# One core: x and u are split into two fp16 parts and transposed by DMA, where TensorE transposed them in f32

## The chip, the core and the metric

The kernel runs on one core of a Trainium2 chip. That core has a matrix engine (TensorE, PE in the profile; PEld is its weight load), a vector engine (VectorE, DVE), an activation engine (ScalarE, ACT), a general engine (GpSimd, POOL) and an engine that here only issues DMA transfers (SyncE, SP). Each executes its own list of instructions in order, and semaphores tie the lists together. The metric is the time of one execution on the device in microseconds (us); less is better.

## The reference

Two stages for 4 batches of 768 tokens. The first is attention in 8 heads of 64, in which a query sees only the keys of its own bucket; the second mixes channels and tokens of the result `x` (768 x 512 for each batch):

```python
    mask = q_bucket[:, :, :, None] == k_bucket[:, :, None, :]
    scores = scale * np.matmul(q, k.transpose(0, 1, 3, 2))
    scores = np.where(mask, scores, -1000000000.0)
    ...
    x = np.ascontiguousarray(attn_out.transpose(0, 2, 1, 3)).reshape(B, S, H * D)
    ...
    theta = x @ w_theta
    cos_t, sin_t = (np.cos(theta), np.sin(theta))
    zr = x * cos_t
    zi = x * sin_t
    yr = np.einsum('ts,bsd->btd', w_tok_r, zr)
    yi = np.einsum('ts,bsd->btd', w_tok_i, zi)
    u = x + (yr + yi)
    return (u + np.maximum(u @ w_ch, 0.0)).astype(np.float32)
```

All inputs are float64 or float32 arrays of random numbers; the output is float32.

## The kernel before

**Tiling.** The 768 tokens of a batch are 6 tiles of 128 partitions, the 512 channels 4 chunks of 128. Products are made nearly exact by splitting each operand into a high and a low part and summing three products (high x high, high x low, low x high). A "tile" of a product is thus 4 chunks x 3 terms = 12 matmuls of 128x128 by 512 columns for theta (`ps_th`) and for the channel product (`ps_r`), and 6 token tiles x 2 (real, imaginary) x 3 = 36 for the token product (`py`).

**Attention** (`prep_qk`, `prep_v`, `maxima`, `step`): for each head `sq` are scores whose row maxima DVE takes (`mc`, L721), `st` the scores once more in transposed form, `pf` the exponential on ACT (L799), two parts `p` of it on ACT (L805) and POOL (L811), and `po` the product with the values. DVE divides and writes the result into `x` (`rc` L849, `x` L855).

**The second stage** (`moe`), for each batch: `transposed` has PE transpose a 128x512 tile of x into PSUM (`pt_x`, L900, 4 instructions), ACT copies it as the high part (`h_x`, L905, format fp32r), DVE subtracts for the low part (`l_x`, L909); `project` multiplies by the theta weights (`ps_th`); ACT rounds to whole turns (`n`, L941), DVE takes the rest (L944), ACT and DVE the magnitude; `trig` takes cosine and sine for 3 tiles at once (L966, L967), DVE multiplies by x (`f`, L978), and `z` is split in two fp16 parts (L983, L985, L989). `token` sums `py`, DVE adds it to x (L1017, this is u), u is transposed and split as x was (`pt_u`, `h_u`, `l_u`), multiplied by the channel weights (`ps_r`), DVE takes the ReLU and adds (L1024), and SP stores (L1027).

**Weights** arrive as 64-bit floats and are rebuilt as f32 on DVE and ACT (`widened`, L381, L385, L390, L391). The two token weights come in 6 row tiles `t0` to `t5` (`prep_wtok`), get a power-of-two scale for each row (L354 to L356, L394), are transposed on PE (`pwt`, L439) and split into fp16 (`wtk`). The theta and channel weights (`wth`, `wch`) are held in fp32r, split chunk by chunk (`split_weight`).

**What sets the order.** `issue_all` builds each engine's list before the program is made: a list scheduler with its own durations takes, on each engine that it holds to be free, the ready operation of least priority number. The priority numbers are the constants at the end of the file (`TH0` for theta, `Y0` for py, `W0` for token weights, and so on), in units of one attention step. `Slot` objects are buffers: `xt` (2) holds a transposed and split tile, `m` (4 banks of PSUM) the accumulators of the attention and of `moe`, `tmp` (3) f32 tiles. Theta and py of a batch are put among the attention of the next; those of batch 3 stand alone at the end.

Of the kernel before, what the change touches and what calls it, by code (L numbers as in the profile page):

```python
# [34 lines left out]
def lsh_attention_moe_kernel(ctx: ExitStack, tc: tile.TileContext, q, k, v, proj, w_theta, w_tok_r, w_tok_i, w_ch, aff, out):  # L35
    nc = tc.nc
# [312 lines left out]
    sinv = const.tile([P, T], F32, name="sinv")  # L349
# [14 lines left out]
    def widened(srcs, n, nm, tag, prio, am=None, stage="x", by=1.0, scaled=None):  # L364
# [5 lines left out]
        def load():  # L370
# [31 lines left out]
    wready = {"th": [], "ch": [], "tk": []}

    def split_weight(src, dst, c, cols, nm, tag, stage, prio, by=1.0):
        lo, n = cols
        k_ = n / DM
        t, g, sz = widened([src[c * P : (c + 1) * P, lo : lo + n].bitcast(U32)], n, f"{nm}{c}_{lo}", tag, prio, stage=stage, by=by)
        dh, dl = (d[:, c, lo : lo + n] for d in dst)
        h_ = op("wh", prio, on("ACT", 100 + 420 * k_, lambda: ACT.activation(dh, t["w"][:, 0], AF.Copy)), [g], [sz])

        def low(eng):
            return lambda: eng.tensor_tensor(dl, t["w"][:, 0], dh.bitcast(F32), ALU.subtract)

        wready[nm].append(h_)
        wready[nm].append(op("wl", prio, {"POOL": (130 + 1100 * k_, low(POOL)), "DVE": (65 + 535 * k_, low(DVE))}, [h_], [sz]))

    def prep_wtok(tau, prio):
        am = const.tile([P, 1], F32, name=f"wam_{tau}")
        def scale(t):
# [5 lines left out]
            S, f"t{tau}", "z0" if tau >= LATE else f"z{tau % 2}", prio, am, "z1" if tau >= LATE else "x", scaled=scale,  # L425
# [3 lines left out]
        for c0 in range(0, 2 * T, TC):  # L429
            def chunk(c0=c0):  # L430
# [12 lines left out]
                wready["tk"].append(op("wtl", prio, on("DVE", 66 + 133.5 * TC, lambda: DVE.tensor_tensor(lo, u["pt"], hi, ALU.subtract)), [e], [sm_]))  # L443
# [419 lines left out]
    def moe(b, G):  # L863
# [28 lines left out]
        def transposed(src, nm, prio, deps, kind):  # L892
            u = {}
            sm_, make = acc(f"pt_{nm}", kind)
            sxt = Slot("xt")

            def tr():
                u["pt"] = make().rearrange("p (c n) -> p c n", c=NC)
                for c in range(NC):
                    PE.transpose(u["pt"][:, c], src()[:, c * P : (c + 1) * P], ident)  # L900

            def high():
                u["hi"] = mp.tile([P, NC, P], F32R, tag="h" + sxt.tag, name=f"h_{nm}")
                u["lo"] = mp.tile([P, NC, P], F32R, tag="l" + sxt.tag, name=f"l_{nm}")
                ACT.activation(u["hi"], u["pt"], AF.Copy)  # L905
# [3 lines left out]
            c = op("xl", prio, on("DVE", 600, lambda: DVE.tensor_tensor(u["lo"], u["pt"], u["hi"].bitcast(F32), ALU.subtract)), [b_], [sm_, sxt])  # L909
# [22 lines left out]
        for tt in range(T):  # L932
            def theta(tt=tt):
                prio = G + at("TH0", b) + at("TH1", b) * tt
                u, deps, sxt = transposed(lambda: tl[b][:, tt], f"x{b}_{tt}", prio, xready[b][tt // 2], "x")
                res, pe, sm_ = project(u, deps, sxt, wth, f"th{b}_{tt}", prio, wready["th"], "p")
                s1 = Slot("tmp")

                def turns():
                    u["n"] = tmp(f"n_{b}_{tt}", s1)  # L940
                    ACT.activation(u["n"], res["ps"], AF.Identity, bias=magic)  # L941
# [16 lines left out]
        for t0, t1 in GROUPS[GR1 if b == B - 1 else GR]:  # L958
            def trig(t0=t0, t1=t1):
# [4 lines left out]
                def go():  # L964
                    c_, s_ = (t["zw"][r][:, sl].rearrange("p t d -> p (t d)") for r in range(2))
                    ACT.activation(c_, c_, AF.Sin, bias=hpi, scale=-TURN)  # L966
                    ACT.activation(s_, s_, AF.Sin, scale=-TURN)  # L967
# [210 lines left out]
```

## Time and profile before

| what | us |
|---|---|
| time, median of 3 runs | 806.96 |
| the 3 runs | 805.57, 808.13, 806.96 |
| the profiled execution, its own time | 808.25 |
| its span, first to last instruction | 806.1 |
| PE, busy in the span | 732.8 |
| ACT, busy | 552.1 |
| DVE, busy | 547.6 |
| POOL, busy | 473.9 |

The span is 2.15 us shorter than the execution's own time. A busy PE is not one at its peak: consecutive matmuls overlap, so the mean duration of one is longer than the distance from one to the next. That distance is read from the chain of waits, which counts each stretch once. The granted PE clock was 0.972 of full speed in the mean.

### The profile page before, as it was taken

The page shows a single profiled execution, that of the slowest core. Times are in us where ns is not written, and L with a number is a line of the kernel's source. Part 1 is how long each engine was busy: PE and PEld are TensorE (multiplying, and loading weights), DVE is VectorE, ACT ScalarE, POOL GpSimd, SP SyncE. Part 2 cuts the span into 40 slices and gives each one's busy share as a digit, 9 for nine tenths or more (in the row PEclk, how much of TensorE's full clock was granted, in tenths as well). Part 3 has the DMA queues.
Part 4 walks back from the last instruction along what each step waited for, and adds up shares of the span by engine and source line. Part 5 has one row for each costly group of instructions (what it writes and reads, how often), then busy time and mean ns, then how long its engine had stood idle before and what let it go on. Part 6 is the DMA issues. An engine that isn't in the chain of part 4 may idle for free.

```text
span 806.1 us, 17749 instructions
## 1 busy us (share of the span) xinstructions
PE 732.8 (91%) x6760; PEld 472.2 (59%) x6760; DVE 547.6 (68%) x1027; ACT 552.1 (68%) x983; POOL 473.9 (59%) x496
## 2 busy tenths in 40 slices
PE   2578697779899999999899999999899999999998
PEld 1246465447555656767556666668556666675456
DVE  7989999895688746685786655684696755236413
ACT  5488899888787754898887564778796654657101
POOL 4168889687659724695569653765667564631200
PEclk9988999999899999999899999999899999999999
DMA  7354454433103232323003220332004110000002
GB/s 219 87 152 145 135 160 143 130 88 84 38 15 109 66 98 66 98 74 88 27 21 103 80 70 29 101 84 69 21 21 115 46 47 14 15 14 1 1 1 78
DMA packets 35268, 59.52 MB, mean 74 GB/s; under 512 B 7456, under 2 KB 24944, under 8 KB 35184
## 3 DMA queue, kind: packets, MB, share of 16 engines
q1 hardware_dynamic: 35184, 58.40, 25.3%
q8 instruction: 53, 0.87, 0.5%
q14 instruction: 31, 0.25, 0.1%
HBM read 32.51 MB, written 6.29 MB: 48 GB/s over the span
## 4 chain that ended last, share of the span: by engine, by line
PE 69%; DVE 13%; ACT 7%; issue 3%; POOL 3%; DMA 3%; SPq 1%; ACTq 0%; DVEq 0%; POOLq 0%
PE py L78 21%; PE st L78 12%; PE po L78 11%; PE ps_r L78 8%; PE ps_th L78 8%; PE sq L78 5%; DVE mc L721 4%; ACT pf L799 3%; DVE hl L577 1%; POOL p L811 1%; ACT p L805 1%; PE pt_u L900 1%; DVE f L978 1%; PE pt_x L900 1%; PE pb L78 1%
## 5 line engine op out<-in xcount | busy, mean ns | idle before, releaser
L811 POOL TENSOR_TENSOR p<-pf,p 128x512 f16<-128x512 f32 x288 | 365.0, 1290 | 143.3 <-ACT p L805 80.0
L78 PE MATMUL py<-z,wtk 128*128 128x512 f16 x864 | 218.2, 385 | 0.5 <-DVE z L989 0.3
L721 DVE TENSOR_REDUCE mc<-sq 128x1 f32<-128x512 f32 (+1 forms) x288 | 188.8, 681 | 40.8 <-PE sq L78 40.0
L799 ACT ACTIVATE pf<-st 128x512 f32<-128x512 f32 x288 | 163.1, 592 | 75.7 <-PE st L78 66.2
L78 PE MATMUL st<-qt,kt 108*128 108x512 f16 (+3 forms) x768 | 169.9, 338 | 24.7 <-ACT pf L799 23.2
L805 ACT ACTIVATE p<-pf 128x512 f16<-128x512 f32 x288 | 170.8, 628 | 18.2 <-PE po L78 16.8
L78 PEld LDWEIGHTS <-p 128*128 128x128 f16 x3456 | 141.6, 99 | 44.1 <-issue 11.0
L78 PE MATMUL po<-vv,p 128*128 128x65 f16 (+1 forms) x3456 | 154.7, 195 | 3.0 <-POOL p L811 2.4
L78 PEld LDWEIGHTS <-wtk 128*128 128x128 f16 x864 | 82.5, 99 | 85.5 <-issue 9.7
L78 PE MATMUL sq<-kt,qt 108*128 108x256 f16 (+1 forms) x384 | 105.7, 337 | 27.1 <-DVE mc L721 18.2
L78 PEld LDWEIGHTS <-kt 108*128 108x128 f16 (+1 forms) x768 | 72.2, 101 | 74.9 <-issue 42.1
L989 POOL TENSOR_TENSOR z<-f,z 128x512 f16<-128x512 f32 x38 | 50.9, 1348 | 71.2 <-ACT z L983 54.2
L78 PEld LDWEIGHTS <-qt 108*128 108x128 f16 x384 | 35.5, 101 | 51.0 <-issue 30.0
L78 PE MATMUL ps_th<-wth,h_x 128*128 128x512 f32 x192 | 64.2, 416 | 1.2 <-DVE z L944 0.8
L78 PE MATMUL ps_r<-wch,h_u 128*128 128x512 f32 x192 | 63.0, 409 | 0.8 <-DVE l_u L909 0.8
L978 DVE SCALAR_TENSOR_TENSOR f<-x,zsc,z 128x512 f32<-128x512 f32 x48 | 56.2, 1208 | 8.8 <-ACT z L966 4.8
L1017 DVE SCALAR_TENSOR_TENSOR x<-py,sw,x 128x512 f32<-128x512 f32 x24 | 17.9, 746 | 48.7 <-PE py L78 48.7
L1024 DVE SCALAR_TENSOR_TENSOR x<-ps_r,x 128x512 f32<-128x512 f32 x24 | 16.6, 691 | 47.3 <-PE ps_r L78 47.3
L905 ACT ACTIVATE h_u<-pt_u 128x512 fp32r<-128x512 f32 x24 | 14.1, 592 | 50.4 <-PE pt_u L900 33.8
L78 PEld LDWEIGHTS ps_th<-wth,h_x 128*128 128x128 f32 x192 | 36.3, 194 | 10.6 <-DVE z L944 1.3
L78 PEld LDWEIGHTS ps_r<-wch,h_u 128*128 128x128 f32 x192 | 35.0, 188 | 10.5 <-DVE l_u L909 2.4
L577 DVE SCALAR_TENSOR_TENSOR hl<-raw,sc,hl 128x768 f16<-128x768 f32 x32 | 40.2, 1266 | 0.0
(128 smaller groups left out, 904.3 us busy)
## 6 DMA issues: line engine op xcount, KB each, us to landing
raw<-in_q_dram SPq DMA_DIRECT2D x16, 384.0 KB
raw<-in_k_dram SPq DMA_DIRECT2D x16, 384.0 KB
vb<-in_v_dram SPq DMA_DIRECT2D x16, 384.0 KB
out_dram<-x SPq DMA_DIRECT2D x24, 256.0 KB
qt<-hl SPq DMA_DIRECT2D x31, 192.0 KB
kt<-hl SPq DMA_DIRECT2D x31, 192.0 KB
w_t<-in_moe_w_tok_r_dram SPq DMA_DIRECT2D x6, 768.0 KB
w_t<-in_moe_w_tok_i_dram SPq DMA_DIRECT2D x6, 768.0 KB
```

What stands on the lines that cost most here:

```text
L78: PE.matmul(out_, l, r, start=start, stop=stop, skip_group_check=True)
L577: DVE.scalar_tensor_tensor(t["hl"][:, 1, i], t["raw", i], t["sc"][:, 2 + i : 3 + i], t["hl"][:, 0, i], ALU.mult, ALU.subtract)
L721: DVE.tensor_reduce(col()[:, cs], u["sq"], AX.X, ALU.max)
L799: ACT.activation(wide("pf", spf, F32), u["st"], AF.Exp, scale=1.0 / (UNIT * math.sqrt(D)))
L805: ACT.activation(o_, u["pf"], AF.Copy)
L811: return lambda: eng.tensor_tensor(wide("p2", sp2, F16), u["pf"], u["p1"], ALU.subtract)
L900: PE.transpose(u["pt"][:, c], src()[:, c * P : (c + 1) * P], ident)
L905: ACT.activation(u["hi"], u["pt"], AF.Copy)
L978: DVE.scalar_tensor_tensor(u["f"], tl[b][:, tt], zsc[:, b : b + 1], t["zw"][r][:, tt], ALU.mult, ALU.mult)
L989: return lambda: eng.tensor_tensor(t["z"][r, 1][:, tt], u["f"], t["z"][r, 0][:, tt], ALU.subtract)
L1017: DVE.scalar_tensor_tensor(tl[b][:, to], res["py"], t["sw"][:, to : to + 1], tl[b][:, to], ALU.mult, ALU.add)
L1024: DVE.scalar_tensor_tensor(tl[b][:, to], r_["ps"], 0.0, tl[b][:, to], ALU.max, ALU.add)
```

## The change

1. **x and u are split before they are transposed.** `transposed` writes into a tile `s` two fp16 parts of the scaled 128x512 tile: the high part on ACT or DVE, the low part (scaled x minus high part) on DVE. Both read x in SBUF. One DMA transpose on SP's queue then turns `s` (128 rows of 8 blocks of 128) into `t`. PE's transposes, their PSUM banks and their copies are gone. `s` has 2 buffers (`xt`), `t` 2 more (`xd`).
2. **Theta and channel weights become scaled fp16.** `prep_weight` gathers all of a weight in f32, takes its sum of magnitudes, a power-of-two scale from one small matmul (`pw`), and then splits into fp16 on ACT and DVE. The scales go into `mg`, `ns`, `su` and `qu`, small DVE operations once for each batch.
3. **ReLU on ACT.** `relu` (ACT, from PSUM, scaled) writes an f32 tile, `fin` (DVE or POOL) adds it to u.
4. **Late token weights.** Tiles `t4` and `t5` have buffers of their own (`wx`, `wz`), and py of batch 0 waits, for each output tile, only for the weights of that tile.
5. **The order is made anew**: other constants, and an offset for each kind of operation and batch (`OFF`).

```diff
-    wth = [wp.tile([P, NC, DM], F32R, name=f"wth{i}") for i in range(2)]
-    wch = [wp.tile([P, NC, DM], F32R, name=f"wch{i}") for i in range(2)]
+    wth = [wp.tile([P, NC, DM], F16, name=f"wth{i}") for i in range(2)]
+    wch = [wp.tile([P, NC, DM], F16, name=f"wch{i}") for i in range(2)]
...
-            S, f"t{tau}", "z0" if tau >= LATE else f"z{tau % 2}", prio, am, "z1" if tau >= LATE else "x", scaled=scale,
+            S, f"t{tau}", "wz" if tau >= LATE else f"z{tau % 2}", prio, am, "wx" if tau >= LATE else "x", scaled=scale,
...
-            def tr():
-                u["pt"] = make().rearrange("p (c n) -> p c n", c=NC)
-                for c in range(NC):
-                    PE.transpose(u["pt"][:, c], src()[:, c * P : (c + 1) * P], ident)
...
-            a = op("xtr", prio, on("PE", 440, tr), deps, [sm_, sx])
-            b_ = op("xh", prio, on("ACT", 480, high), [a], [sm_, sxt])
-            c = op("xl", prio, on("DVE", 600, lambda: DVE.tensor_tensor(u["lo"], u["pt"], u["hi"].bitcast(F32), ALU.subtract)), [b_], [sm_, sxt])
+                    if e == "ACT":
+                        ACT.activation(u["s"][:, 0], src(), AF.Copy, scale=sc())
+                    else:
+                        DVE.tensor_scalar(u["s"][:, 0], src(), sc(), None, ALU.mult)
...
+                DVE.scalar_tensor_tensor(u["s"][:, 1], src(), sc(), u["s"][:, 0], ALU.mult, ALU.subtract)
...
+                nc.sync.dma_start_transpose(u["t"].rearrange("p i c n -> p (i c) n"), u["s"].rearrange("p i d -> p (i d)"))
+
+            a = op("xh", prio, {"ACT": (580, high("ACT")), "DVE": (340, high("DVE"))}, deps, [sx, sxs])
+            c = op("xl", prio, on("DVE", 610, low), [a], [sx, sxs])
+            d = op("xturn", prio, on("SP", [(600, 500000)], turn), [c], [sxs, sxt])
...
-                        mm(res["ps"], u[a][:, c], w[bb][:, c], n == 0, n == len(terms) - 1)
+                        mm(res["ps"], u["t"][:, a, c], w[bb][:, c], n == 0, n == len(terms) - 1)
...
-                    DVE.scalar_tensor_tensor(tl[b][:, to], r_["ps"], 0.0, tl[b][:, to], ALU.max, ALU.add)
+                    ACT.activation(v_["r"], r_["ps"], AF.Relu, scale=t["qu"][:, to : to + 1])
...
+                    return lambda: eng.tensor_tensor(tl[b][:, to], v_["r"], tl[b][:, to], ALU.add)
...
-LATE = 6
+LATE = 4
```

**The order, place 1: the last token weight on DVE.** In the names the first number is the batch: `mc_0_6` is head 6 of batch 0, `wf_t5` token weight tile 5. Before, its rebuilding stands among the maxima of batch 0:

```order
L721 TENSOR_REDUCE mc_0_6_1818<-sq_0_6_6_1862 128x1
L381 TENSOR_SCALAR wf_t5_1755<-w64_t5_1752 128x1536
L516 SCALAR_TENSOR_TENSOR mt_0_3_1790<-pm_0_3_1871,vsc_105,mh_0_3_1879 1x2x64
L385 SCALAR_TENSOR_TENSOR wf_t5_1755<-w64_t5_1752,wf_t5_1755 128x1536
L721 TENSOR_REDUCE mc_0_6_1818<-sq_0_6_7_1869 128x1
```

In the changed kernel it stands about 80 rows later, with the maxima of batch 1 and the first tile of x:

```order
L608 SCALAR_TENSOR_TENSOR hl_1_1_2160<-raw1_1_1_2080,sc_1_1_2161,hl_1_1_2160 128x768
L386 TENSOR_SCALAR wf_t5_2633<-w64_t5_2630 128x1536
L880 RECIPROCAL rc_0_7_1_2838<-po_0_7_0_2587 128x6
L752 TENSOR_REDUCE mc_1_1_2713<-sq_1_1_3_2828 128x1
L886 SCALAR_TENSOR_TENSOR x_0_828<-po_0_7_0_2587,vinv_109,rc_0_7_1_2838 128x6x64
L917 TENSOR_SCALAR sw_0_2727<-sinv_101,zinv_111 128x1
L965 SCALAR_TENSOR_TENSOR s_x0_0_2852<-x_0_828,zsc_112,s_x0_0_2852 128x512
```

Tile 5 (and the two channel chunks that stood ahead of theta) has moved behind the end of batch 0's attention.

**Place 2: SP's list at the end.** `t_x3_0` is the transposed tile 0 of x of batch 3, `t_u3_0` that of u, `out_0_dram` the output. Of the changed kernel:

```order
L969 DMA_TRANSPOSE t_x3_0_11280<-s_x3_0_11270 128x8x128
L969 DMA_TRANSPOSE t_x3_1_11305<-s_x3_1_11272 128x8x128
L1098 DMA out_0_dram<-x_2_6168 128x512
L969 DMA_TRANSPOSE t_x3_2_11332<-s_x3_2_11312 128x8x128
L969 DMA_TRANSPOSE t_x3_3_11360<-s_x3_3_11325 128x8x128
L969 DMA_TRANSPOSE t_x3_4_11396<-s_x3_4_11385 128x8x128
L969 DMA_TRANSPOSE t_x3_5_11418<-s_x3_5_11402 128x8x128
L969 DMA_TRANSPOSE t_u3_0_11591<-s_u3_0_11580 128x8x128
L969 DMA_TRANSPOSE t_u3_1_11605<-s_u3_1_11596 128x8x128
L969 DMA_TRANSPOSE t_u3_2_11654<-s_u3_2_11639 128x8x128
```

Before, SP's list held only stores there. With two buffers for `t`, `t_x3_2` waits until PE has done the 12 matmuls of `ps_th3_0`, and so on by twos.

**Place 3: DVE's last rows.** Before, the last u tiles are split long after their `py` is done:

```order
L1024 SCALAR_TENSOR_TENSOR x_3_9078<-ps_r3_3_11879,x_3_9078 128x512
L909 TENSOR_TENSOR l_u3_1_11903<-pt_u3_1_11871,h_u3_1_11902 128x512
L1024 SCALAR_TENSOR_TENSOR x_3_9078<-ps_r3_2_11898,x_3_9078 128x512
L909 TENSOR_TENSOR l_u3_0_11922<-pt_u3_0_11844,h_u3_0_11921 128x512
L1024 SCALAR_TENSOR_TENSOR x_3_9078<-ps_r3_1_11917,x_3_9078 128x512
L1024 SCALAR_TENSOR_TENSOR x_3_9078<-ps_r3_0_11936,x_3_9078 128x512
```

In the changed kernel each `py` is followed by its split, and three additions stand at the end:

```order
L1081 SCALAR_TENSOR_TENSOR x_3_9044<-py_3_5_11768,sw_3_11153,x_3_9044 128x512
L965 SCALAR_TENSOR_TENSOR s_u3_5_11819<-x_3_9044,su_3_11154,s_u3_5_11819 128x512
L1094 TENSOR_TENSOR x_3_9044<-rl_3_3_11832,x_3_9044 128x512
L1094 TENSOR_TENSOR x_3_9044<-rl_3_4_11847,x_3_9044 128x512
L1094 TENSOR_TENSOR x_3_9044<-rl_3_5_11864,x_3_9044 128x512
```

Between the end of `py_3_5` and the first matmul of `ps_r3_5` PE's list now holds `ps_r3_3` and `ps_r3_4`, 24 matmuls; before, `ps_r` of all six tiles stood behind the last `py`.

More of the change, by code (lines that the diff above doesn't have):

```diff
@@ L362, in root_scale, with widened @@
         DVE.tensor_scalar(r.bitcast(U32), inv.bitcast(U32), MASK, None, ALU.bitwise_xor)
-    def widened(srcs, n, nm, tag, prio, am=None, stage="x", by=1.0, scaled=None):
+    def widened(srcs, n, nm, tag, prio, am=None, stage="x", by=1.0, scaled=None, into=None, hold=()):
         m = len(srcs)
@@ L398, in widened @@
             "DVE": (60 + 535 * k_, lambda: DVE.tensor_tensor(t["f"], t["f"], t["sg"], ALU.mult)),
-        }, [d, t["abs"]], [sz])
+        }, [d, t["abs"]], [sz] + hold)
         return t, g, sz
[L402 to L415, printed above, removed]
+    wready = {"th": [], "ch": [], "tk": [[] for _ in range(T)]}
@@ new lines, in prep_weight, with into, joined, total @@
+    def prep_weight(src, dst, nm, n, tag, stage, prio, step, by=1.0):
+        u = {}
+        sf, sa = Slot("wf"), Slot("m")
+        sums = const.tile([P, NC * DM // n], F32, name=f"wsum_{nm}")
+        col = const.tile([P, 1], F32, name=f"wcol_{nm}")
+        done = []
+        for c in range(NC):
+            for lo in range(0, DM, n):
+                def into(c=c, lo=lo):
+                    if "f" not in u:
+                        u["f"] = mp.tile([P, NC, DM], F32, tag=sf.tag, name=f"wf_{nm}")
+                    return u["f"][:, c, lo : lo + n]
+                i = (c * DM + lo) // n
+                t, g, sz = widened(
+                    [src[c * P : (c + 1) * P, lo : lo + n].bitcast(U32)], n, f"{nm}{c}_{lo}", tag, prio + step * i, sums[:, i : i + 1], stage=stage, by=by, into=into, hold=[sf]
+                )
+                done.append(g)
+        def joined():
+            DVE.tensor_reduce(col, sums, AX.X, ALU.add)
+            DVE.tensor_scalar(col, col, 2.0**-14, col, ALU.mult, ALU.mult)
+            DVE.tensor_scalar(col, col, 2.0**-14, None, ALU.mult)
+        def total():
+            u["pa"] = bank(sa, [P, 1], f"pw_{nm}")
+            mm(u["pa"], ones, col, True, True)
+        last_ = prio + step * (NC * DM // n - 1)
+        a = op("wcol", last_, on("DVE", 450, joined), done)
+        a = op("wall", last_, on("PE", 60, total), [a], [sa])
+        r = op("wcsc", last_, on("DVE", 520, lambda: root_scale(u["pa"], csc[nm], cinv[nm])), [a], [sa])
+        for c in range(NC):
+            dh, dl = (d[:, c] for d in dst)
+            h_ = op("wh", last_ + 0.01 * c, on("ACT", 600, lambda c=c, dh=dh: ACT.activation(dh, u["f"][:, c], AF.Copy, scale=csc[nm])), [r], [sf])
+            wready[nm].append(h_)
+            wready[nm].append(op("wl", last_ + 0.01 * c, on("DVE", 600, lambda c=c, dh=dh, dl=dl: DVE.scalar_tensor_tensor(dl, u["f"][:, c], csc[nm], dh, ALU.mult, ALU.subtract)), [h_], [sf]))
@@ L1036, in lsh_attention_moe_kernel @@
         prep_wtok(tau, W0 + WS * tau if tau < LATE else WL0 + WLS * (tau - LATE))
-    for c in range(NC):
-        split_weight(w_theta, wth, c, (0, DM), "th", "z0", "x", WTH + WTS * c, 1.0 / TWO_PI)
-        for half in range(2):
-            split_weight(w_ch, wch, c, (half * DM // 2, DM // 2), "ch", "tmp", "tmp", WC + WCS * (c + 0.5 * half))
+    prep_weight(w_theta, wth, "th", DM, "z0", "x", WTH, WTS, 1.0 / TWO_PI)
+    prep_weight(w_ch, wch, "ch", DM // 2, "tmp", "tmp", WC, WCS * 0.5)
     g = 0
@@ L1089 @@
 GR = 0
-PEN = 0.031
+PEN = 0.904
 GR1 = 0
```

224 lines of the change are left out of this document (132 added, 92 removed), and 38 rows, old and new, of the table OFF.

## The prediction

> **What bounds the kernel now.** I read the busy times first, then the chain of waits by engine, then the busy times stage by stage.
>
> ```profile
> PE 732.8 (91%) x6760; PEld 472.2 (59%) x6760; DVE 547.6 (68%) x1027; ACT 552.1 (68%) x983; POOL 473.9 (59%) x496
> ```
> ```profile
> PE 69%; DVE 13%; ACT 7%; issue 3%; POOL 3%; DMA 3%; SPq 1%; ACTq 0%; DVEq 0%; POOLq 0%
> ```
> ```profile
> core 0: us, PE busy (x) PEld busy (x) DVE busy (x) ACT busy (x) POOL busy (x), PEclk, DMA share, GB/s
> 0.00:189.00 189.00, 134.70 (x1452) 86.22 (x1453) 168.81 (x325) 151.51 (x273) 134.27 (x142) 0.94 0.47 140
> 189.00:371.00 182.00, 175.32 (x1675) 114.00 (x1675) 128.47 (x247) 134.63 (x249) 116.72 (x125) 0.98 0.26 73
> 371.00:548.00 177.00, 173.92 (x1673) 113.05 (x1672) 118.60 (x230) 126.32 (x227) 112.16 (x120) 0.98 0.24 66
> 548.00:713.00 165.00, 161.27 (x1538) 105.73 (x1536) 95.91 (x180) 110.37 (x196) 99.04 (x103) 0.98 0.15 40
> 713.00:806.10 93.10, 87.58 (x430) 53.18 (x428) 35.85 (x48) 29.24 (x43) 11.71 (x9) 0.99 0.05 18
> ```
>
> The first line says that PE leads; the last two show that the mean hides two kinds of stages. The first theta product starts at 189 us:
>
> ```profile
> 188.95 5.69 PE ps_th L78 x24
> ```
>
> Ahead of it PE idles 54.3 us and DVE is busy 168.81 of 189 (89%): weights are being rebuilt there, and DVE is the bound. Behind it PE is busy 98% (stages two to four) and 94% (the tail), and DVE and ACT stand at 74% or less. So work taken off PE counts nearly whole behind 189 us and not at all ahead of it, and DVE work taken out counts only ahead of it.
>
> **The change part by part.**
>
> *PE: transposes and fp32r products go.* Pieces of the chain:
>
> ```profile
> 761.59 0.44 PE pt_u L900 x4
> 762.03 7.12 PE py L78 x33
> ...
> 790.05 0.44 PE pt_u L900 x4
> 790.49 11.95 PE ps_r L78 x51
> ```
>
> Four transposes hold PE 0.44 us for each of 48 tiles. An fp32r matmul follows the last after 11.95 / 51 = 0.234 us, an fp16 one after 7.12 / 33 = 0.216 us, with the same 128x512 shape; 12 of them save 0.22 us. Together 0.66 us a tile, 31.5 us for all 48. All of these stand behind 189 us: 36 tiles among attention, at 98%, save **23.6 us**, and 12 in the tail **7.9 us**. Bounds: nothing (if another engine takes over) and 31.5 together.
>
> *The front.* The last token tile and two chunks of the channel weights are rebuilt later (place 1 of the order). In DVE time, ahead of the first split of x:
>
> ```profile
> L394 DVE SCALAR_TENSOR_TENSOR wf_t<-wf_t,scw 128x1536 f32<-128x1536 f32 x6 | 12.7, 2110 | 0.0
> L385 DVE SCALAR_TENSOR_TENSOR wf_t<-w_t,wf_t 128x1536 uint32<-128x1536 uint32 x6 | 12.3, 2042 | 0.0
> L443 DVE TENSOR_TENSOR wtk<-pwt,wtk 128x512 f16<-128x512 f32 x18 | 11.6, 682 | 1.5 <-ACT wtk L442 1.4
> L381 DVE TENSOR_SCALAR wf_t<-w_t 128x1536 uint32<-128x1536 uint32 x6 | 6.4, 1067 | 0.0
> L385 DVE SCALAR_TENSOR_TENSOR wf_ch<-w_ch,wf_ch 128x256 uint32<-128x256 uint32 x8 | 5.5, 688 | 0.1
> L381 DVE TENSOR_SCALAR wf_ch<-w_ch 128x256 uint32<-128x256 uint32 x8 | 4.6, 569 | 0.0
> L573 DVE TENSOR_SCALAR hl<-raw,sc 128x768 f16<-128x768 f32 x11 | 7.8, 724 | 0.0
> ```
>
> One token tile is 2.11 + 2.04 + 1.07 + 3 x 0.68 = 7.3 us, two chunks 2 x (0.69 + 0.57) = 2.5, less two copies `hl` that move from ACT to DVE, 1.4: 8.4 us. I take **8 us**, since DVE is the bound there. Bounds: nothing, if ACT (151.51 of 189) is what ends last; 15, if also the chain's longest wait ahead of 189 us goes, since the loads of `t1` and `t4` now stand at the very start:
>
> ```profile
> 45.20 6.58 DMA w_t<-in_moe_w_tok_i_dram
> ```
>
> The deferred 10 us of DVE land where DVE has 26% free.
>
> *DVE elsewhere.* Low parts now read two SBUF tiles instead of PSUM:
>
> ```profile
> L909 DVE TENSOR_TENSOR l_u<-pt_u,h_u 128x512 fp32r<-128x512 f32 x24 | 16.4, 686 | 8.5 <-ACT h_u L905 8.3
> L978 DVE SCALAR_TENSOR_TENSOR f<-x,zsc,z 128x512 f32<-128x512 f32 x48 | 56.2, 1208 | 8.8 <-ACT z L966 4.8
> ...
> L1024 DVE SCALAR_TENSOR_TENSOR x<-ps_r,x 128x512 f32<-128x512 f32 x24 | 16.6, 691 | 47.3 <-PE ps_r L78 47.3
> ```
> ```profile
> 728.62 0.75 DVE L978 SCALAR_TENSOR_TENSOR f<-x,zsc,z 128x512 f32<-128x512 f32 x1 [2.50 <-ACT z L966]
> ```
>
> L978 is the nearest row for such a form: 0.75 us alone, 1.21 in the mean while POOL works. The 48 low parts thus cost 3 to 25 us more than at 0.69, the 19 final additions that stay on DVE up to 10 more, 15 high parts at most 0.72 each. The upper ends sum to 46 us, some 12 a batch: DVE goes from 118.60 to about 131 of a period that shrinks to 169 (78%), still under PE. ACT gains 24 ReLUs, and has 15 splits fewer. Hidden, then; but fuller engines make later partners, and I put **2 us** on it (bounds 0 and 20: the three periods staying as they are).
>
> *The DMA transpose* is an operation that the trace does not show. Its bytes are 128 x 1024 x 2 = 256 KB. The nearest row by size is a store of 256 KB:
>
> ```profile
> L1027 SPq DMA_DIRECT2D out_dram<-x x24: 332/344/528, 285.1 to 803.2; - x24
> ```
>
> The last is issued at 803.2 and the span ends at 806.1: 2.9 us. No row excludes less. For the other end I suppose that it is cut into pieces of one row of one block, 256 bytes:
>
> ```profile
> q1 hardware_dynamic: 35184, 58.40, 25.3%
> ```
>
> 25.3% of 16 x 806.1 us over 35184 packets is 93 ns each; 1024 pieces on 16 engines are 64 x 93 ns = 5.9 us, with 2.9 of fixed time 8.8 us. I take L = 4 us, near the store.
>
> What hides it: `t` has two buffers, so the transfer for tile k+2 starts when the product of tile k is done, and PE's cover is what its list holds until the product of tile k+2. Counting that list with the steps above: 3.6 to 6 us among attention (mean some 4.6), where two such links follow one another in a batch, three batches. In the tail it is less: one product and a few attention matmuls, 3.4 us, then one product alone, 12 x 0.216 = 2.6 us. At the end `py_3_5` is followed by u (0.75 by its row, L1017), a high part (0.59, L905), a low part (0.75), the transfer, covered by two products of 2.6: 5.2 - 2.1 leaves 3.1 for the transfer.
>
> ```profile
> L1017 DVE SCALAR_TENSOR_TENSOR x<-py,sw,x x24: 720/750/753, 248.8 to 784.7; 128x512 f32<-128x512 f32 x24
> ```
> ```profile
> L905 ACT ACTIVATE h_u<-pt_u 128x512 fp32r<-128x512 f32 x24 | 14.1, 592 | 50.4 <-PE pt_u L900 33.8
> ```
>
> So the loss is 6 (L - 4.6) + (L - 3.4) + (L - 2.6) + (L - 3.1), each only where positive: nothing to speak of at 3, **2.9 us** at 4, 17 at 6, 42 at 8.8. SP's list is in order: behind a waiting transpose stand loads and `qt`/`kt` pieces of the next heads, and PE's `sq` and `st` wait for those; this is in the upper end.
>
> The Trainium skill, VectorE: DVE Perf Modes, section The three transpose paths, gives 1309 ns for a DMA transpose of one 128x128 block; eight in sequence would be an estimate of 10.5 us, and the loss by the formula above 58 us. The same skill's Advanced Engine Details and Errata, section X-Bar Transpose (TRN2), has such transfers as fast as plain ones, 350 to 400 GB/s, an estimate of 0.7 us of data. No trace here shows either, and they differ by the whole gain.
>
> *The rest of the end.* ReLU on ACT ahead of the addition is one step more behind the last matmul, **0.7 us** (the 0.69 us of an ACT read of such a bank, below, and 0.75 for 0.69 on DVE). In the tail only two `py` instead of three or four share each new `z`; PE may wait **1 us** more there.
>
> ```profile
> L941 ACT ACTIVATE n<-ps_th,magic 128x512 f32<-128x512 f32 x24 | 16.6, 690 | 13.6 <-PE ps_th L78 12.2 <-DVE wch L412 0.9
> ```
>
> Sum: 808.25 - 23.6 - 7.9 - 8 + 2 + 2.9 + 0.7 + 1 = 775.4 for an execution like the profiled one, which lay 1.3 above the median; the prediction is **774 us**.
>
> **The rivals.**
>
> *A: slower, by the transpose.* If L is over 8.1 us, the loss outweighs the 35.8 us that are left of the 39.5 saved after the other costs (2 + 0.7 + 1). Place: `ps_th` and `ps_r` waiting for a DMA, in the tail and in every batch. At the upper end 8.8 it is 774 - 2.9 + 42 = 813. For it: 256-byte pieces, and a queue that carries attention loads too. Against: the break-even is close to the upper end of what rows allow. By the Trainium skill's 1309 ns a block (VectorE: DVE Perf Modes, The three transpose paths) this rival would come out at about 829.
>
> *B: half the gain.* DVE, fuller and contending with POOL, ends last in the periods, or the front does not shorten because the second pair's `raw` loads now stand behind 6 weight loads. With 10 us lost there and 5 on transposes of L = 5: about 789. For it: DVE at 78% is an average, and the 0.75 against 1.21 us of L978 shows the contention.
>
> *C: the front gives more.* With the 6.58 us wait and the idle time around the weights gone, 15 to 20 in place of 8, transposes hidden whole: about 762.
>
> **How the numbers follow.** The forecast (766 to 783) has a chance of 0.5, B (783 to 804) 0.22, C 0.17, A 0.11. A range from 757 to 800 leaves out most of A, a corner of B and a little of C, 2 in 10. A measurement can tell about 0.3% from no change, 2.4 us: faster 0.87, same 0.03, slower 0.10.
>
> **What would show it.** Right: no `pt_x` and `pt_u`; `ps_th` and `ps_r` at 0.216 a step; PE busy near 700; the first `ps_th` near 181; periods near 169; `t` landing some 4 us after issue. Wrong: PE's waits led by a DMA at `ps_th` (A), DVE over 85% in the middle stages or PE waiting for `s`'s low part (B). The forecast falls first with L, then with the front.

## The result, and the profile after

| | before | after |
|---|---|---|
| time, median of 4 runs of each (us); before: the three above and one more | 806.66 | 777.59 |
| the runs, lowest to highest | 805.57 to 808.13 | 776.79 to 779.74 |
| ratio after / before | | 0.9643 (95%: 0.9617 to 0.9668) |
| span of the profiled execution | 806.1 | 777.9 |

The changed kernel is 29 us faster, 3.6%; 774 us was predicted, 777.59 measured. Busy times and the chain of waits by engine, of the kernel after:

```profile
PE 698.8 (90%) x6572; PEld 400.5 (51%) x6572; DVE 592.1 (76%) x1086; ACT 564.1 (73%) x999; POOL 475.8 (61%) x490
```
```profile
PE 50%; DVE 23%; ACT 11%; DMA 6%; issue 4%; SPq 2%; POOL 2%; DVEq 0%; ACTq 0%; POOLq 0%
```

PE has 34.0 us less (732.8 before) and stands on 50% of the chain in place of 69%; DVE has 44.5 us more and went from 13% to 23%. The gain came, and DVE now ends many more waits. By stages, cut at the first `ps_th` of each batch:

```profile
core 0: us, PE busy (x) PEld busy (x) DVE busy (x) ACT busy (x) POOL busy (x), PEclk, DMA share, GB/s
0.00:182.80 182.80, 133.11 (x1443) 85.53 (x1444) 165.12 (x329) 146.06 (x266) 127.34 (x137) 0.91 0.47 140
182.80:362.90 180.10, 171.08 (x1665) 97.53 (x1664) 147.23 (x282) 146.41 (x272) 125.33 (x128) 0.99 0.39 97
362.90:529.60 166.70, 161.55 (x1604) 93.45 (x1603) 132.44 (x236) 126.90 (x226) 113.49 (x118) 1.00 0.36 88
529.60:687.20 157.60, 152.95 (x1488) 88.25 (x1489) 108.55 (x191) 112.95 (x195) 97.24 (x100) 0.98 0.28 60
687.20:777.90 90.70, 80.14 (x376) 35.71 (x376) 38.74 (x51) 31.81 (x44) 12.45 (x9) 1.00 0.22 53
```

The front lost 6 us (189 to 182.8), the middle, from the first `ps_th` to that of batch 3, 20 (524.0 to 504.4), the tail 2.4 (93.1 to 90.7). The 20 are uneven: the three periods between the first `ps_th` of one batch and of the next lost 1.9, 10.3 and 7.4 us, and by the counts in the rows they lost 10, 69 and 50 matmuls, though 48 transposes went from each: the new order also moves PE's work from one period to another. In the first of them DVE is busy 82% and ACT 81%. The transposes, as SP issued them, their queue, the low parts, and PE's waits for a transfer:

```profile
L969 SPq DMA_TRANSPOSE t_x<-s_x x24: 1232/1251/2604, 178.3 to 699.3; - x24
```
```profile
q1 hardware_dynamic: 85872, 70.99, 35.5%
```
```profile
L965 DVE SCALAR_TENSOR_TENSOR s_x<-x,zsc,s_x 128x512 f16<-128x512 f32 x24 | 24.6, 1040 | 3.3 <-ACT s_x L959 2.9
L965 DVE SCALAR_TENSOR_TENSOR s_u<-x,su,s_u 128x512 f16<-128x512 f32 x24 | 22.6, 943 | 7.3 <-ACT s_u L959 7.2
```
```profile
PE sq L76 <- DVE mc L752: 15.4, 28, 1.7
...
PE ps_th L76 <- DMA t_x<-s_x: 1.9, 2, 1.3
...
PE st L76 <- DMA qt<-row: 1.3, 2, 1.1
...
PE ps_r L76 <- DMA t_u<-s_u: 0.6, 1, 0.6
PE sq L76 <- DMA kt<-rows: 0.5, 1, 0.5
```

SP is held 1.25 us by an issue in the median (the line has minimum, median and maximum in ns), and the queue moved 50688 packets more, 1056 for each of the 48 transposes. The prediction's supposition of 1024 small pieces was near; their price was not: the packets' time rose from 25.3% of 16 x 806.1 us to 35.5% of 16 x 777.9, which is 23 ns for each packet more, where 93 had been taken for the upper end. PE waited 2.5 us in all for a transpose. The end, from the chain:

```profile
764.99 2.60 PE ps_r L76 x12
...
767.61 3.08 DMA t_u<-s_u
...
770.74 2.78 PE ps_r L76 x12
```

This last transfer lands 3.08 us after its issue, close to the 2.9 of a plain store of that size. It is issued 2.6 us before the end of the 24 matmuls that cover it, and PE then waits 0.6 us.

### The profile page after: what moved, and what is told of

The parts are those of the page before. It is cut to its first block, busy times and chain, and to the rows that moved or that the text cites. A ratio compares the mean times of both kernels' runs of the same rounds, so it can differ in the third digit from the quotient of the medians.

```text
span 777.9 us, 17533 instructions
## 1 busy us (share of the span) xinstructions
PE 698.8 (90%) x6572; PEld 400.5 (51%) x6572; DVE 592.1 (76%) x1086; ACT 564.1 (73%) x999; POOL 475.8 (61%) x490
## 3 DMA queue, kind: packets, MB, share of 16 engines
q1 hardware_dynamic: 85872, 70.99, 35.5%
## 4 chain that ended last, share of the span: by engine, by line
PE 50%; DVE 23%; ACT 11%; DMA 6%; issue 4%; SPq 2%; POOL 2%; DVEq 0%; ACTq 0%; POOLq 0%
PE py L76 16%; PE st L76 9%; PE po L76 8%; PE ps_r L76 6%; DVE mc L752 6%; PE ps_th L76 5%; PE sq L76 4%; ACT pf L830 2%; DMA t_x<-s_x 2%; ACT p L836 2%; DVE hl L608 1%; ACT z L1047 1%; POOL p L842 1%; DVE s_x L965 1%; SPq L709 1%
## 5 line engine op out<-in xcount | busy, mean ns | idle before, releaser
L76 PE MATMUL py<-z,wtk 128*128 128x512 f16 x864 | 212.2, 378 | 4.7 <-ACT z L1047 1.9
L76 PE MATMUL st<-qt,kt 98*128 98x256 f16 (+3 forms) x768 | 169.1, 332 | 15.6 <-ACT pf L830 13.7
L76 PE MATMUL sq<-kt,qt 108*128 108x256 f16 (+1 forms) x384 | 107.1, 340 | 28.1 <-DVE mc L752 15.4
L76 PEld LDWEIGHTS <-wtk 128*128 128x128 f16 x864 | 82.0, 98 | 90.7 <-issue 8.1
L1053 POOL TENSOR_TENSOR z<-f,z 128x512 f16<-128x512 f32 x33 | 46.3, 1415 | 45.0 <-ACT z L1047 42.6
L76 PE MATMUL ps_r<-wch,t_u 128*128 128x512 f16 x288 | 68.7, 388 | 0.9 <-DMA t_u<-s_u 0.6
L76 PE MATMUL ps_th<-wth,t_x 128*128 128x512 f16 x288 | 66.5, 384 | 2.3 <-DMA t_x<-s_x 1.9
L76 PEld LDWEIGHTS <-qt 108*128 108x128 f16 x384 | 34.8, 101 | 56.6 <-issue 24.9
L1042 DVE SCALAR_TENSOR_TENSOR f<-x,zsc,z 128x512 f32<-128x512 f32 x48 | 49.5, 1072 | 6.3 <-ACT z L1030 4.4
L76 PEld LDWEIGHTS <-t_x 128*128 128x128 f16 x288 | 27.5, 99 | 37.9 <-DMA t_x<-s_x 5.9
L76 PEld LDWEIGHTS <-t_u 128*128 128x128 f16 x288 | 28.4, 100 | 35.5 <-issue 3.4
L1094 DVE TENSOR_TENSOR x<-rl,x 128x512 f32<-128x512 f32 x19 | 16.1, 846 | 35.7 <-ACT rl L1091 35.5
L959 ACT ACTIVATE s_u<-x,su 128x512 f16<-128x512 f32 x20 | 14.4, 720 | 38.8 <-DVE x L1081 38.1
```

Source lines behind the costliest of these rows:

```text
L76: PE.matmul(out_, l, r, start=start, stop=stop, skip_group_check=True)
L959: ACT.activation(u["s"][:, 0], src(), AF.Copy, scale=sc())
L1042: DVE.scalar_tensor_tensor(u["f"], tl[b][:, tt], zsc[:, b : b + 1], t["zw"][r][:, tt], ALU.mult, ALU.mult)
L1053: return lambda: eng.tensor_tensor(t["z"][r, 1][:, tt], u["f"], t["z"][r, 0][:, tt], ALU.subtract)
L1094: return lambda: eng.tensor_tensor(tl[b][:, to], v_["r"], tl[b][:, to], ALU.add)
```

## The experiments

Differences in us are differences of ratios times 806.7. Each ratio has an interval of 0.002 to 0.007 to either side, 2 to 5 us, that of the changed kernel 0.0025, and the kernel before ran at medians of 803.2 to 806.7 in the five sets of runs, so less than 5 us between kernels of different sets is not told apart by the times. Apart from `e4b_wl`, `e8_small_early` and `e5_no_off` the kernels keep the order of every list (`e6_before_fp16` but for two rows).

| run | what is done | ratio (95%) | us |
|---|---|---|---|
| `e1_pe_back` | PE's transposes added to after | 0.9859 (0.9806 to 0.9912) | after + 17 |
| `e6_before_fp16` | fp16 products in before | 0.9865 (0.9815 to 0.9914) | before - 11 |
| `e2_low_twice` | low parts twice in after | 1.0076 (1.0048 to 1.0103) | after + 35 |
| `b_low_twice` | low parts twice in before | 1.0150 (1.0095 to 1.0206) | before + 12 |
| `e11_low_zero` | after without low parts | 0.9696 (0.9634 to 0.9759) | after + 4 |
| `e3_turn_twice` | each transpose twice | 1.1107 (1.1040 to 1.1175) | after + 118 |
| `e13_turn_halves` | each transpose in halves | 0.9880 (0.9830 to 0.9931) | after + 19 |
| `e14_ring3` | three buffers `s` and `t` | 0.9699 (0.9672 to 0.9726) | after + 5 |
| `e12_front_add` | 12 more DVE steps in the front | 0.9853 (0.9801 to 0.9906) | after + 17 |
| `e4b_wl` | t5 rebuilt early again | 1.0083 (1.0052 to 1.0114) | after + 35 |
| `e8_small_early` | small DVE steps of batch 3 earlier | 0.9925 (0.9900 to 0.9950) | after + 23 |
| `e5_no_off` | no table of offsets | 1.0217 (1.0158 to 1.0277) | after + 46 |

**What PE's work is worth.** `e1_pe_back` has PE transpose each tile once more into the bank that the product then overwrites; nothing reads it.

```diff
+                        for c in range(NC):
+                            PE.transpose(res["ps"][:, c * P : (c + 1) * P], src()[:, c * P : (c + 1) * P], ident)
```

> The changed kernel with PE's four f32 transposes of each x and u tile put back as dead work: they write the bank that the product behind them overwrites, nothing reads them, nothing else and no order changes. Theory 1 (behind the front PE is the bound, and the gain is PE work that went): 48 x 0.44 = 21 us more, less what falls into PE's waits in the tail: 793 to 799 us, ratio to before 0.983 to 0.991. Theory 2 (the gain comes from the new order, PE has room): under 5 us more, below 783.

48 x 0.44 = 21 us of PE cost 17, 0.8 for each (0.6 to 1 within the intervals), as the first theory has it. `e6_before_fp16` makes only the format of the theta and channel products fp16, without scales, in the kernel before.

```diff
-    wth = [wp.tile([P, NC, DM], F32R, name=f"wth{i}") for i in range(2)]
-    wch = [wp.tile([P, NC, DM], F32R, name=f"wch{i}") for i in range(2)]
+    wth = [wp.tile([P, NC, DM], F16, name=f"wth{i}") for i in range(2)]
+    wch = [wp.tile([P, NC, DM], F16, name=f"wch{i}") for i in range(2)]
```

> The kernel before with theta and channel weights and the split parts of x and u held in plain fp16 instead of fp32r, unscaled, so with less exact products; the order stays. This is the format alone. Theory 1: 576 matmuls at a distance of 0.216 instead of 0.234 us save 10.4 us, nearly all behind the front: 796 to 799. Rival (what PE saves there it waits for elsewhere): 803 or more.

It gave 11, where 48 x 0.22 = 10.4 was worked out. The two together are 28 us, with an interval of some 6 to either side, as much as the whole change. So the rest of it, gains and losses together, comes to about nothing within that interval; one of the two was measured in the old order and one in the new, and that they add up is assumed.

**DVE.** `e2_low_twice` writes each low part twice, `b_low_twice` does the same with `l_x` and `l_u` before, and `e11_low_zero` puts a memset in the place of the subtraction, so that the low parts of x and u are zero.

```diff
-                DVE.scalar_tensor_tensor(u["s"][:, 1], src(), sc(), u["s"][:, 0], ALU.mult, ALU.subtract)
+                for _ in range(2):
+                    DVE.scalar_tensor_tensor(u["s"][:, 1], src(), sc(), u["s"][:, 0], ALU.mult, ALU.subtract)
```

> The changed kernel with every low part of x and u written twice by DVE (the same values again), 48 more DVE instructions of about 1 us, no other change of order. Theory 1 (DVE is hidden behind PE outside the front): only the links of the tail show, 2 to 6 us: 780 to 784. Rival B (DVE, at 81% in the two middle stages, is what ends last there): 12 us a batch come through, 800 or more.

```diff
-lambda: DVE.tensor_tensor(u["lo"], u["pt"], u["hi"].bitcast(F32), ALU.subtract)
+lambda: [DVE.tensor_tensor(u["lo"], u["pt"], u["hi"].bitcast(F32), ALU.subtract) for _ in range(2)]
```

> The kernel before, with each low part l_x and l_u written twice: 48 more DVE instructions of some 0.69 us, 33 us of DVE in all, in the same order. In the changed kernel 47 us more of the same kind cost 34 us, 0.7 us for each. Theory (the kernel before had DVE time to spare, which the change used up): at most 0.3 us for each, ratio 1.000 to 1.012. Rival (these lists never had slack at this place: any longer low part is paid at 0.6 or more in both kernels): ratio 1.025 to 1.035.

```diff
-                DVE.scalar_tensor_tensor(u["s"][:, 1], src(), sc(), u["s"][:, 0], ALU.mult, ALU.subtract)
+                DVE.memset(u["s"][:, 1], 0.0)
```

> The changed kernel with the low parts of x and u left out: a memset to zero takes the place of the subtraction, so DVE loses some 0.7 us in each of 48 places (34 us), in the same order. Theory (DVE's length stands behind the products, in both directions): 0.5 us or more gained for each, ratio 0.925 to 0.944 (746 to 761 us). Rival (the price is one-sided: shorter than now, another engine's wait takes its place): a gain of at most 6 us, ratio 0.957 to 0.966.

The low parts of u in `e2_low_twice` (those of x take 46.1 us), PE's waits there and the third period behind the front; then one of the two groups of memsets of `e11_low_zero`, which are alike (busy us, mean ns):

```profile
L966 DVE SCALAR_TENSOR_TENSOR s_u<-x,su,s_u 128x512 f16<-128x512 f32 x48 | 48.1, 1002 | 8.2 <-ACT s_u L959 7.2
```
```profile
PE sq L76 <- DVE mc L752: 28.3, 40, 2.9
...
PE ps_th L76 <- DMA t_x<-s_x: 6.8, 4, 3.0
```
```profile
549.60:715.00 165.40, 154.04 (x1487) 88.16 (x1487) 121.21 (x208) 111.60 (x191) 97.88 (x99) 0.98 0.28 58
```
```profile
L965 DVE MEMSET s_x<- 128x256 uint32 x24 | 6.5, 272 | 2.2 <-DMA t_x<-s_x 2.2
```

In the changed kernel 47 us more of DVE cost 35, 0.74 for each; in the kernel before, 33 us cost 12, 0.37 for each; 34 us less gained nothing. (Before, a low part also holds a PSUM bank, so 0.37 is the price of both.) The first theory on `e2_low_twice`, DVE hidden behind PE, missed, and so did both forecasts for `b_low_twice`: 1.015 lies between them. For `e11_low_zero` the rival holds: the price is one-sided. What is added to DVE delays the maxima `mc`, and PE's `sq` waits 28.3 us for them in place of 15.4. That is 13 of the 30 us by which the span is longer; PE's waits for `t` grew by 6 (from 2.5 to 8.3, since each transfer also starts 1 us later) and its busy time by 8.5. So the 35 us are the price of DVE time and of later transfers together, and no run separates the two. Nor does the price follow DVE's share: the third period, where DVE was busy 69%, grew by 7.8 us (157.6 to 165.4), the first, at 82%, by 10.8.

**The transfer.** `e3_turn_twice` issues each transpose twice into the same tile; `e13_turn_halves` issues the high and the low part apart; `e14_ring3` gives `s` and `t` a third buffer.

```diff
+                nc.sync.dma_start_transpose(u["t"].rearrange("p i c n -> p (i c) n"), u["s"].rearrange("p i d -> p (i d)"))
```

> The changed kernel with each DMA transpose issued twice in a row to the same tile; the product waits for both. The trace of the changed kernel has 1.25 us for the issue and 3.1 us from issue to landing, so the landing moves from 3.1 to about 4.4 us. Theory 1 (the prediction's formula, links of 3.4, 2.6 and 3.1 us of cover in the tail and 4.6 in the batches): 3 to 4 us more, 780 to 782. Rival A (SP's list is the edge: attention loads behind the transposes are late too): 10 us or more, 788 and up.

SP's issues at the end, PE's waits, and the busy times:

```profile
878.77 1.23 SPq L969 DMA_TRANSPOSE t_u<-s_u  x1
881.85 1.23 SPq L970 DMA_TRANSPOSE t_u<-s_u  x1
```
```profile
PE ps_th L76 <- DMA t_x<-s_x: 43.0, 16, 5.0
PE ps_r L76 <- DMA t_u<-s_u: 26.9, 12, 4.2
```
```profile
PE 736.7 (82%) x6572; PEld 407.5 (46%) x6572; DVE 583.5 (65%) x1086; ACT 565.8 (63%) x999; POOL 472.1 (53%) x490
```

The second issue starts 3.08 us after the first, the time that one needs to land, so L (from issue to landing) is 6.2 us, not the 4.4 expected, and SP is held 4.3 us. PE waits 69.9 us for transposes (2.5 in the changed kernel) and is busy 37.9 us longer with the same 6572 matmuls, at a granted clock of 0.928 in the mean: 105 of the 116 us by which the span is longer. Theory 1 missed; rival A's forecast holds, but the run changes L and SP's time at once.

```diff
-                nc.sync.dma_start_transpose(u["t"].rearrange("p i c n -> p (i c) n"), u["s"].rearrange("p i d -> p (i d)"))
+                [nc.sync.dma_start_transpose(u["t"][:, i], u["s"][:, i]) for i in range(2)]
```

> The changed kernel with each transpose issued as two, one for the high and one for the low part (4 blocks of 128x128 each, different halves of t): the same bytes, the same order. Theory (SP's 1.25 us of issuing is a fixed time of each, and the pair lands some 1.2 us later than the one did): the price of L that the doubled transpose showed, some 38 us for 1 us, gives 25 to 50 us more, ratio 0.995 to 1.03. Rival (issue and landing go with the number of blocks, 0.6 us and 2 to 3 us each): within 5 us, ratio 0.958 to 0.971.

SP's issue times of that kernel, the last pair on SP and in the chain, and PE's waits:

```profile
L969 SPq DMA_TRANSPOSE t_x<-s_x x48: 1188/1216/2153, 176.2 to 715.1; - x48
```
```profile
782.05 2.50 SPq L969 DMA_TRANSPOSE t_u<-s_u  x2
```
```profile
783.36 2.43 DMA t_u<-s_u
```
```profile
PE ps_th L76 <- DMA t_x<-s_x: 9.6, 13, 1.6
...
PE st L76 <- DMA qt<-row: 3.7, 5, 1.2
PE sq L76 <- DMA kt<-rows: 3.5, 4, 1.3
```

Four blocks hold SP 1.22 us where eight held it 1.25: the time is one of each issue. The landing is not: 2.43 us for four blocks, 3.08 for eight. The last pair, issued from 782.05, has landed at 785.79, 3.7 us after. The ratio of 0.988 lies between the two forecasts: the theory has the mechanism, at about half its price. PE waits 7.7 us more for `t_x`, and 5.4 us more (7.2 against 1.8) for the `qt` and `kt` pieces, which SP issues from the same list. These waits are 13 us more; the span gained 15, PE's idle time 11.7 and its busy time 3.0, so some other waits shrank.

```diff
-    u["s"] = mp.tile([P, 2, DM], F16, tag=sxs.tag, name=f"s_{nm}")
+    u["s"] = mp.tile([P, 2, DM], F16, tag=f"sr{next(ring_s) % 3}", name=f"s_{nm}")
...
-    u["t"] = mp.tile([P, 2, NC, P], F16, tag=sxt.tag, name=f"t_{nm}")
+    u["t"] = mp.tile([P, 2, NC, P], F16, tag=f"tr{next(ring_t) % 3}", name=f"t_{nm}")
```

> The changed kernel with three buffers each for s and t in place of two, every list in exactly the same order: only waits of the split for an old transfer and of a transfer for PE's reading of an old t go away. Theory (the ring of two t buffers is what makes the transfers late, as at the very end, where the last one waits for a product): 1.5 to 4 us less, ratio 0.959 to 0.9625. Rival (the transfers are late because of SP's list and of the split on DVE and ACT): within 1 us, ratio 0.963 to 0.9665.

Medians of 777.88 and 777.59 us and spans of 776.2 and 777.9 say that nothing changed; the ratio, above both forecasts, is higher because the kernel before ran at 803.25 on that chip. The gain of the theory did not come, as the rival has it: at the end the transfer now starts as soon as the split is written (765.05 + 0.75 = 765.80), only 0.2 us sooner after it than in the changed kernel (766.62 + 0.75 = 767.37, issue at 767.61).

```profile
765.05 0.75 DVE L965 SCALAR_TENSOR_TENSOR s_u<-x,su,s_u 128x512 f16<-128x512 f32 x1 [0.84 <-ACT s_u L959]
```
```profile
765.86 1.23 SPq L969 DMA_TRANSPOSE t_u<-s_u  x1
```

**The front.** `e12_front_add` repeats a short DVE step of the theta weights; `e4b_wl` puts `t5` back.

```diff
-DVE.tensor_scalar(t["f"].bitcast(U32), t["lo"], 29, 0x40000000, ALU.logical_shift_right, ALU.bitwise_xor)
+[DVE.tensor_scalar(t["f"].bitcast(U32), t["lo"], 29, 0x40000000, ALU.logical_shift_right, ALU.bitwise_xor) for _ in range(4 if nm.startswith("th") else 1)]
```

> The changed kernel with one short DVE step of each theta weight chunk (L386, the shift of the low word, some 0.6 us) executed four times: 12 more DVE instructions, 7 to 8 us of DVE ahead of the first ps_th, and every list otherwise in the same order. Theory (DVE sets the front, and what follows only starts later): first ps_th at 189 to 191 us and a time 6 to 9 us longer, ratio 0.971 to 0.976. Rival 1 (ACT or the loads set the front): less than 3 us longer, ratio under 0.968. Rival 2 (a later first ps_th upsets what follows, as when t5 was put back): 20 us or more, ratio 0.985 or above.

The repeated group (2.6 us for 4 in the changed kernel) and the stages of `e12_front_add`:

```profile
L386 DVE TENSOR_SCALAR wf_th<-w_th 128x512 uint32<-128x512 uint32 x16 | 15.0, 937 | 0.4
```
```profile
0.00:195.10 195.10, 137.57 (x1443) 88.72 (x1444) 175.81 (x341) 147.03 (x266) 127.01 (x137) 0.89 0.44 132
195.10:374.10 179.00, 169.65 (x1664) 97.32 (x1663) 147.23 (x282) 146.43 (x272) 125.72 (x129) 1.00 0.40 98
```

The group has 12.4 us more, not 7 to 8, since a repeat took 1.03 us; the first `ps_th` stands 12.3 us later, and every stage behind it is as long as in the changed kernel, within 1.1 us (one of the four is shown). The ratio is that of rival 2, but the trace shows the theory's mechanism, at a price of 1 for 1. (The medians differ by 16 us, the two profiled executions by 11; the 5 between lie within the interval.)

```diff
-WL0 = 21.841
-WLS = 10.706
+WL0 = 14.0
+WLS = 3.0
```

> The rebuilding of the last token weight t5 is put back ahead of the theta weights on DVE (some 60 rows earlier); everything else is as in the changed kernel, but for what the scheduler moves round it. Theory (the front gained because t5's 7.3 us of DVE left it): first ps_th goes from 183 back to some 190 us, and the time rises by 5 to 8 us: ratio 0.970 to 0.975 (782 to 787 us). Rival (ACT or the loads end last in the front, the deferral brought nothing): first ps_th stays within 1.5 us of 183, ratio within 0.961 to 0.967.

The first `ps_th` of batches 0 and 1 in `e4b_wl`, and a window between them:

```profile
189.98 0.63 PE L76 MATMUL ps_th<-wth,t_x 128*128 128x512 f16 x1
...
389.00 1.24 PE L76 MATMUL ps_th<-wth,t_x 128*128 128x512 f16 x5
```
```profile
210.00:220.00 10.00, 5.39 (x20) 1.87 (x21) 7.82 (x10) 9.59 (x18) 7.25 (x6) 0.50 0.39 78
```

The front is 7.2 us longer, the theory's number. But the first period took 199 us in place of 180: the attention's `sq` and `st` wait for `kt`, ACT and the maxima, PE is busy 54% of these ten us, and the granted clock falls to 0.50 in them. The time forecast, 5 to 8 us, missed. So this run cannot price the deferral alone; it prices the order with it.

**The order.** `e8_small_early` brings the small DVE steps of batch 3 (`su`, `mg`, `ns`, `qu`) some 45 rows forward, with the buffers of `z` taken later; `e5_no_off` empties the table of offsets.

```diff
-        st0 = op("moe", G + at("TH0", b) - 0.5, on("DVE", 800 + 300, start), ([] if b == 0 else alltk) + vready[b] + wready["th"], sz)
+        st0 = op("moe", G + at("TH0", b) - (5 if b == B - 1 else 0.5), on("DVE", 800 + 300, start), ([] if b == 0 else alltk) + vready[b] + wready["th"])
...
-        st2 = op("sback", G + at("Y0", b), on("DVE", 300, back), [st1] + wready["ch"])
+        st2 = op("sback", G + at("Y0", b) - (8 if b == B - 1 else 0), on("DVE", 300, back), [st1] + wready["ch"])
```

> The changed kernel with the small 128x6 scale operations of batch 3 (su, mg, qu, some 1.1 us each beside POOL) some 45 rows earlier on DVE, where they stand between ps_r of batch 2 and ps_th of batch 3 now. Theory (they stand on the path at 675 to 681 us and cost PE its idle time and, through the granted clock, 2.3 us of ps_r2_5): 3 to 5 us less, ratio 0.958 to 0.961. Rival (theta's own split and transposes end last there anyway, and the new order takes it back): ratio 0.963 or more.

```diff
-OFF = {
...
-}
+OFF = {}
```

> The changed kernel without the table of offsets: the same operations, the order that the constants and the scheduler's durations alone give. Theory (the order fits this program's waits closely: two runs in which a few DVE rows were moved lost 18 and 35 us): 20 us or more longer, ratio 0.99 or above. Rival (the offsets only refine): at most 8 us longer, ratio 0.975 or below.

The steps in question, on the chain of the changed kernel:

```profile
678.25 1.05 DVE qu L927
...
679.33 1.08 DVE qu L928
...
684.07 3.04 DMA t_x<-s_x
...
687.16 2.76 PE ps_th L76 x12
```

Moving them made the kernel 23 us slower: the scheduler placed other operations anew too, and the second and third period behind the front grew by 7 and 9 us. The theory missed, and the forecast of the rival holds. Whether the steps themselves cost anything stays open. Without the offsets the same operations are slower than the kernel before; its stages:

```profile
0.00:191.30 191.30, 136.63 (x1455) 87.67 (x1456) 165.35 (x332) 151.81 (x276) 128.11 (x138) 0.89 0.45 138
191.30:382.40 191.10, 175.64 (x1652) 99.12 (x1650) 153.53 (x282) 140.27 (x262) 120.05 (x127) 0.95 0.36 88
382.40:560.80 178.40, 167.53 (x1600) 94.77 (x1599) 129.69 (x238) 126.30 (x224) 116.06 (x118) 0.97 0.34 83
560.80:721.30 160.50, 152.75 (x1500) 87.56 (x1497) 104.56 (x186) 114.11 (x197) 98.91 (x101) 0.99 0.25 57
721.30:821.30 100.00, 84.67 (x377) 36.66 (x375) 39.72 (x50) 32.87 (x45) 11.70 (x9) 0.94 0.20 48
```

8.5, 11.0, 11.7, 2.9 and 9.3 us are lost, some in every stage, as the theory had it. No run was faster than the changed kernel.

## Why the prediction was right, and where its steps were not

The forecast of 774 us was met within 4, and its main step, PE work that goes and counts nearly whole, is the cause that the runs show. Stage by stage the gain came out a little smaller than forecast: of the profiled spans the front lost 6.2 us (8 forecast), the periods 19.6 (21.6: 23.6 less 2), the tail 2.4 (3.3).

- **PE, 31.5 us less**: right. The runs that put one part back or did one part alone give 17 of 21 and 11 of 10.4 us, 28 together.
- **The front, 8 us**: 6 by the trace. That DVE sets it is shown (`e12_front_add`, 1 for 1), and with `t5` put back it is 7.2 longer, what the scheduler moved included. But DVE's busy time in the front fell by only 3.7 us (168.81 to 165.12), not by the 8.4 worked out, and its idle time by 2.5. Part of what came back is in the rows of the front: `hl` high parts take 4.3 us on DVE for 1.8, the sign products of the theta weights 4.4 for 2.5, their low parts 2.7 for 2.0. And the two channel chunks had taken 1.7 us there, not the 2.5 that the means of the whole run gave.
- **Transposes, 2.9 us at L = 4**: L was 3.08 at the end, and PE waited 2.5 us for transfers. That the two sizes agree is luck: at 3.08 the formula gives 0.5, and it is far too flat. It gives 19 us at 6.2 and 2 at 3.7, where 118 and 19 were measured. It counted a late transfer only against the products beside it. The prediction named SP's list but gave it no term: 1.25 us an issue, with the heads' pieces behind it. PE's work at the lower clock after a stall was left out. Rival A's break-even of 8.1 us was therefore far too high: the gain of 29 us would have been gone near 4 us, if SP's hold grows with it as in those runs (an estimate: 19 us for the first 0.65, 118 for 3.1, so 30 to 38 for 1 us). That is the L on which the forecast stood, and by this estimate its chance of 0.11 was too low for this rival. Eight blocks in sequence at the 1309 ns that the Trainium skill (VectorE: DVE Perf Modes, The three transpose paths) gives for one block of 128x128 were the prediction's estimate of 10.5 us; the trace does not agree with that sum, since eight blocks landed 3.08 us after one issue, and no run issues one block alone. That such a transfer is about as fast as a plain one (Advanced Engine Details and Errata, X-Bar Transpose (TRN2), in the Trainium skill) agrees with the 2.9 of the store.
- **DVE "hidden, then", 2 us**: right in size for the work that the change adds, as `e11_low_zero` shows for the low parts. The bound of 46 us was for low parts, high parts and additions, and these took 24 more (14.7, 9.6 and -0.5 by their rows); the rest of the 44.5 had not been listed, among it the steps `su` and `qu`, 8.2 us, and `hl`, 4.9. The 78% under PE was worked out from the second period (118.60 us); the first had 128.47 and got the deferred weights as well, 147.23 of 180.1 us, 82% (the 26% free named for it was ACT's; DVE had 29%). Even so DVE is not what ends that period: in `e11_low_zero`, with DVE busy 138.8 us there, it is as long (180.6 us), so rival B does not show. In the three periods together PE's busy time fell by 24.9 us (23.6 forecast) and its idle time grew by 5.3 (2 forecast). But a share under PE's was no reserve: a further us in each low part cost 0.74 for each us in the mean.
- **The tail, 3.3 us net** (7.9 less 2.9, 0.7 and 1): 2.4. Its PE work fell by 7.4 us (87.58 to 80.14), close to the 7.9 predicted; its idle time grew by 5.0 us (5.5 to 10.6), where 4.6 had been allowed. The parts were not as forecast: PE's `py` waits 4.3 us there for `z` (0.5 before), where 1 had been allowed for fewer `py` on each `z`, and 1.2 us for transfers, where 2.9 had been. The waits for `z` in the tail:

```profile
PE py L76 <- ACT z L1047: 1.9, 2, 1.2
PE py L76 <- POOL z L1053: 1.6, 2, 0.9
PE py L76 <- DVE z L1053: 0.8, 1, 0.8
```

- **The order, priced at nothing**: the step that was missing, and that it did no harm is luck as far as the prediction goes. In the changed kernel the fit of the lists decides more than the whole gain: without the offsets the time is 46 us longer, and the forecast would have been wrong in sign. Whether the constants without offsets, made anew, would do better was not tried.

## What to carry to other kernels

Where PE is the bound, work taken off it counted at 0.8 to 1 in these two runs, but add up what the replacement takes of DVE, of SP's issuing time and of the cover of each transfer, and price the next microsecond there too: here it cost far more than the first. In lists that run in order, an edit's worth is known only with the order it comes with: undo parts with the order held fixed, and treat a change of order as an edit with a price of its own.

## What the runs showed of the hardware beyond this

A short stall can cost PE twice. In the changed kernel PE waited 1.02 us up to 679.32 (for `p` of POOL) and 0.96 us up to 681.01 (for `rc` of DVE). The product of 12 matmuls behind that took 4.92 us where it takes 2.6 to 2.8 elsewhere, with the granted clock at 0.58 in the window. Here the second cost was covered, since `t_x` landed only at 687.1; in `e3_turn_twice`, where PE waited 69.9 us for transposes, PE was busy 37.9 us longer with the same matmuls.

```profile
681.74 4.92 PE L76 MATMUL ps_r<-wch,t_u 128*128 128x512 f16 x12
```
```profile
679.00:687.20 8.20, 6.79 (x49) 3.56 (x50) 4.27 (x9) 1.73 (x3) 2.49 (x3) 0.58 0.34 66
```

At 675 us one DVE step on 128x6 numbers took 1.16 us and another of the same size 0.22. POOL was busy during both, and no run here shows what makes the difference:

```profile
675.32 0.22 DVE L917 TENSOR_SCALAR sw<-sinv,zinv 128x6 f32<-128x6 f32 x1
675.45 1.16 DVE L924 TENSOR_SCALAR su<-tsc,zsc 128x6 f32<-128x6 f32 x1
```
